# Attention and two expert layers on one core: sign masks of the first weight slices in SBUF instead of PSUM, first weight combinations asked for at tile 66, order of the instructions made in four passes

## The chip, the core and the metric

One core of a Trainium2 chip runs the kernel alone. The core has five engines that each work through a list of their own: PE multiplies matrices into PSUM, DVE, ACT and POOL work elementwise, and SP only asks for transfers. POOL works on SBUF alone here; DVE and ACT read and write PSUM too. The metric is the device time of one execution in microseconds (us).

## The reference

```python
q_pool = q.reshape(B, H, S // 2, 2, D).mean(axis=3)          # B 2, H 8, S 1152, D 64
scores = np.matmul(q_pool, k.transpose(0, 1, 3, 2)) / np.sqrt(D)
attn = np.exp(scores - scores.max(-1)); attn = attn / (attn.sum(-1) + 1e-9)
x = np.matmul(attn, v)                                       # then tokens x heads: 1152 x 512
h = x @ moe_w_in;  x = np.maximum(0.01 * h, h) @ moe_w_out   # 512 -> 2048 -> 512
h = x @ moe2_w_in; x = (h * np.tanh(softplus(h))) @ moe2_w_out
```

The four weight matrices arrive as float64, 1152 tokens pass through both layers, and the output is float32.

## The kernel before

**Attention.** Two heads make a pair; eight pairs come one after the other, each as nine tiles of 128 query rows, so there are 72 tiles. A tile n goes through: scores of 128 rows by 1152 keys on PE (L560) into PSUM columns 128 to 1279 for one parity of n and 1280 to 2431 for the other; the row maximum on DVE (L569 over 896 columns, L575 over 256, L580 joins them); the exponential on ACT (L591); nine transposes on PE in three groups (L615); of each group a rounded copy on ACT (L628) and the remainder on DVE (L633), since every product is made of high and low parts; and the product with v on PE (L650). A unit of that product leaves PSUM on ACT (L660), a transfer asked for by SP (L663) and POOL (L664) finish it, and once per pair PE and DVE scale it (L755 to L758). POOL also makes the low parts of the next pair's k, q and v (L394 to L406).

**Expert layers.** Each layer runs over eight slices of 256 hidden columns; i counts the 16 slices. A slice's first product is done in seven smaller products on combined operands (L840, six matmuls each; L845 to L858 finish them), the second product is L915 in layer one and L925 in layer two, summed into Y by DVE (L905, L907). L724 in `last_pair` is the first thing that PE does after the last tile's product with v: it ends the attention.

**Weights.** A slice has four parts b of 128x512 float64. `stage(i, b)` loads a part as pairs of 32-bit words (L786) and makes float32 of it: ACT turns the high word (L787) and the low word (L788) into scaled numbers, DVE takes the sign bit out of the high word (L793) and shifts it into place under the number (L794), and POOL adds the low word (L796). For slices 0 and 1 the sign mask goes, 128 columns at a time, to two strips of PSUM:

```python
strips = [PS[:, c:c + 128].bitcast(I32) for c in (0, 2432)]
```

The kernel itself counts PSUM in banks of 512 columns (`PS[:, 512 * bank[name]:...]`); the two strips lie in the first and the fifth such stretch, beside the columns of the scores. From slice 2 on the mask takes 512 columns at 3584. `convert(i)` makes the combinations of parts 0 and 1 on POOL (L808 and three `minus`) and splits all four parts into high and low.

**Order.** A `Recorder` takes down every operation, works out who depends on whom from the cells that each touches, and `plan` puts all operations in one order. Up to `rec.cut` (tile 63) the order is the one written out by hand in PATTERN; only operations marked loose, such as `stage(0, b)` at tiles 12, 27 and 42, are slipped in where their engine would otherwise idle by the planner's costs. Behind the cut it is a list schedule by due times. Each engine then executes its own list in that order, and waits for other engines where an operation needs it.

Of the kernel before, what the change touches and what calls it, by code (L numbers as in the profile page):

```python
# [26 lines left out]
NPR = B * NPAIR  # L27
# [14 lines left out]
CUT = 63  # L42
# [5 lines left out]
class Op:  # L48
    __slots__ = ("alts", "reads", "writes", "preds", "succs", "due", "n", "loose", "eng", "end", "go")


class Recorder:
# [5 lines left out]
    def __init__(self, nc, file):  # L58
        self.nc, self.file, self.ops, self.open, self.cut, self.free = nc, file, [], None, None, False
        for name in self.ENGINES:  # L60
            setattr(self, name, Proxy(self, name))

    @contextmanager
    def unit(self):
        assert self.open is None
        self.open = []
        yield
        made, self.open = self.open, None
        if made:
            self.add([(made[0][0], [c for m in made for c in m[1]], sum(m[2] for m in made),  # L70
                       sum(m[2] for m in made[:-1]) + made[-1][3])],
                     [x for m in made for x in m[4]], [x for m in made for x in m[5]])

    @contextmanager
    def loose(self):

        self.free = True
        yield
        self.free = False

    def add(self, alts, reads, writes):
        op = Op()
        op.alts, op.reads, op.writes, op.preds, op.succs = alts, reads, writes, set(), []
        op.n, op.eng, op.due, op.loose = len(self.ops), None, 0.0, self.free
        self.ops.append(op)

    def call(self, name, method, args, kw):
        frame = sys._getframe(2)
        while frame.f_code.co_filename != self.file:
            frame = frame.f_back  # L90
        outs = [kw[k] for k in ("out", "accum_out") if k in kw] or list(args[:1])
        ins = [v for k, v in kw.items() if k not in ("out", "accum_out")] + list(args[1 if args and "out" not in kw else 0:])
        outs = [x for x in outs if hasattr(x, "partition_size")]
        ins = [x for x in ins if hasattr(x, "partition_size")]
        eng = self.ENGINES[name]
        occ, fin = self.cost(eng, method, outs, ins, kw)
        reads = [c for x in ins for c in self.cells(x)]
        writes = [c for x in outs for c in self.cells(x)]
        if method == "matmul" and not kw.get("start"):
            reads = reads + writes  # L100
        made = (eng, [(name, method, args, kw, frame.f_lineno)], occ, fin, reads, writes)
        if self.open is not None:
            self.open.append(made)
        else:
            self.add([made[:4]], reads, writes)

    @staticmethod
    def cost(eng, method, outs, ins, kw):
# [56 lines left out]
    def plan(self):  # L165
# [17 lines left out]
        at = 0.0  # L183
        for op in self.ops:
            op.due = at
            if op.alts[0][0] == "PE":
                at += op.alts[0][2]
        back = dict.fromkeys(("PE", "DVE", "ACT", "POOL", "SP"), at + 9000)
# [3 lines left out]
        def latest(op):  # L192
            eng, _, occ, fin = op.alts[0]
            if eng != "PE":
                op.due = at + 3000
            for s in op.succs:
                op.due = min(op.due, s.due - (occ if eng == "PE" and s.alts[0][0] == "PE" else fin + self.SYNC))
            heapq.heappush(heap, (-op.due, -op.n, op))

        for op in self.ops:  # L200
            if not wants[op]:
                latest(op)
        while heap:
            op = heapq.heappop(heap)[2]
            eng, _, occ, _ = op.alts[0]
            op.due = min(op.due, back[eng] - occ)
            if eng != "PE":
                back[eng] = op.due
            for p in op.preds:
                wants[p] -= 1  # L210
                if not wants[p]:
                    latest(p)
        free = dict.fromkeys(("PE", "DVE", "ACT", "POOL", "SP"), 0.0)
        order = []

        def ready(op, eng):
            t = 0.0
            for p in op.preds:
                t = max(t, p.go + p.alts[0][2] if p.eng == eng == "PE" else p.end + self.SYNC)
            return t  # L220

        def place(op, alt):
            eng, calls, occ, fin = alt
            op.eng, op.go = eng, max(free[eng], ready(op, eng))
            op.end = op.go + fin
            free[eng] = op.go + occ
            order.append((op, calls))

        def force(op):
            for p in sorted(op.preds, key=lambda p: p.n):  # L230
                if p.eng is None:
                    force(p)
            place(op, op.alts[0])

        loose = []
        for op in self.ops[:self.cut]:
# [3 lines left out]
            for p in sorted(op.preds, key=lambda p: p.n):  # L240
                if p.eng is None:
                    force(p)
            eng = op.alts[0][0]
            start = max(free[eng], ready(op, eng))
            found = True
            while found:
                found = False
                for l in loose:
                    if l.eng is None and l.alts[0][0] == eng and all(p.eng for p in l.preds):
                        if max(free[eng], ready(l, eng) + 300) + l.alts[0][2] <= start + SLIP:  # L250
                            place(l, l.alts[0])
                            found = True
                            break
            place(op, op.alts[0])
            loose = [l for l in loose if l.eng is None]
        done = len(order)
        rest = [op for op in self.ops if op.eng is None]
        left = {op: sum(p.eng is None for p in op.preds) for op in rest}
        waiting = {op for op in rest if not left[op]}
        while waiting:  # L260
            by = {}
            for op in waiting:
                eng = op.alts[0][0]
                by.setdefault(eng, []).append((max(free[eng], ready(op, eng)), op.due, op.n, op))
            best = []
            for eng, ops in by.items():
                first = min(ops)
                t0 = max(first[0], free[eng])
                near = [x for x in ops if x[0] <= t0 + 5]
                pick = min(near, key=lambda x: x[1:3])  # L270
                soon = [x for x in ops if x[0] <= t0 + LOOK * pick[3].alts[0][2] and x[1] < pick[1] - 1000]
                if soon:
                    pick = min(soon, key=lambda x: x[1:3])
                best.append((pick[0], pick[2], pick[3]))
            _, _, op = min(best)
            place(op, op.alts[0])
            waiting.discard(op)
            for s in op.succs:
                if s in left:
                    left[s] -= 1  # L280
                    if not left[s]:
                        waiting.add(s)
        assert len(order) == len(self.ops)
        return order[:done] + sorted(order[done:], key=lambda x: x[0].go)

    def emit(self):
        lines = {}
        for op, calls in self.plan():
            for name, method, args, kw, line in calls:
# [15 lines left out]
def tile_attention_moe_moe(  # L305
# [65 lines left out]
    strips = [PS[:, c:c + 128].bitcast(I32) for c in (0, 2432)]  # L371
# [400 lines left out]
    def stage(i, b):  # L772
# [23 lines left out]
        nc.gpsimd.tensor_tensor(out=ai, in0=ai, in1=v[:, :, 0], op=ALU.add)  # L796

    def convert(i):

        if i >= NI:  # L800
            return
        wi, wo, a = WI[i % 2], WO[i % 3], wa[i % 2]
# [11 lines left out]
        split([wi[:, A12:S1, h] for h in range(2)], d2)  # L814
        for f in range(2):
            stage(i, 2 + f)
            split([wo[:, h, f] for h in range(2)], a[2 + f])
# [219 lines left out]
    with tc.manual_schedule():  # L1037
# [91 lines left out]
        assert not pvq and not prep  # L1129
        while xq:  # L1130
# [42 lines left out]
```

## Time and profile before

| | |
|---|---|
| device time, median of 3 runs | 661.79 us (661.2 to 662.08) |
| the profiled execution, device time | 661.79 us |
| its span, first to last instruction | 660.0 us |
| PE idle in the span | 23.2 us |
| mean granted TensorE clock | 0.997 of full speed |

The span is what the trace covers; the 1.79 us between it and the device time lie around it. Busy time of an engine is the time in which at least one of its instructions runs, and PE's ends are modelled, so the last two rows say where PE had nothing to do, and not that it ran at its peak elsewhere.

### The profile page before, as it was taken

What the parts mean: (1) busy time and instruction counts of PE and PEld (TensorE: products, weight loads), DVE (VectorE), ACT (ScalarE), POOL (GpSimd) and SP (SyncE); (2) the same over time, 40 slices, a digit from 0 to 9 for tenths busy, and PEclk for the clock granted to TensorE, in tenths of its full rate; (3) what the DMA queues carried; (4) which work ended last, traced back from release to release, by engine and by line L of the source; (5) the groups of instructions that cost most, each with busy time, mean ns of one, the idle gap of its engine ahead of it and who ended that gap; (6) DMA issues with size and microseconds to landing.
All of it is one profiled execution on the core that took longest, in us unless ns stands there. A gap on an engine that the chain in (4) does not pass through costs nothing.

```text
span 660.0 us, 11899 instructions
## 1 busy us (share of the span) xinstructions
PE 636.8 (96%) x4179; PEld 587.2 (89%) x4179; DVE 505.1 (77%) x1072; ACT 493.8 (75%) x1051; POOL 468.2 (71%) x450
## 2 busy tenths in 40 slices
PE   7899999999999988899999999999999999999997
PEld 5799889998999976789999999999999989999996
DVE  5889889998999988767677676678867766767454
ACT  6889889999999977867767766578776767576430
POOL 6957486888888653898777887669766797677200
PEclk9999999999999989999999999999999999999999
DMA  4424233333232222122332231322212232231003
GB/s 122 139 82 152 69 98 107 102 112 85 83 86 77 56 69 68 44 69 97 97 128 96 96 128 66 128 65 65 66 64 97 96 103 90 96 97 65 1 0 144
DMA packets 18172, 57.79 MB, mean 88 GB/s; under 512 B 2368, under 2 KB 4928, under 8 KB 18112
## 3 DMA queue, kind: packets, MB, share of 16 engines
q1 hardware_dynamic: 16768, 52.18, 24.4%
q0 software_dynamic: 1120, 4.59, 3.0%
q8 instruction: 33, 0.54, 0.3%
q14 instruction: 27, 0.22, 0.1%
q10 hardware_dynamic: 224, 0.26, 0.1%
HBM read 47.71 MB, written 2.36 MB: 76 GB/s over the span
## 4 chain that ended last, share of the span: by engine, by line
PE 87%; ACT 5%; DVE 4%; issue 2%; POOL 1%; DMA 1%; SPq 0%; DVEq 0%; ACTq 0%; POOLq 0%
PE PS L840 26%; PE PS L925 15%; PE PS L915 13%; PE PS L560 11%; PE PS L650 10%; PE PS L615 9%; ACT F L591 2%; PE PS L955 2%; DVE R L633 1%; POOL R L394 1%; ACT R L628 1%; DVE F L569 1%; DMA I<-in_kT_dram 1%; PE PS L755 0%; POOL R L406 0%
## 5 line engine op out<-in xcount | busy, mean ns | idle before, releaser
L840 PE MATMUL PS<-R 128*128 128x288 f32 x1344 | 203.9, 295 | 1.3 <-ACT F L591 1.1
L840 PEld LDWEIGHTS PS<-R 128*128 128x128 f32 x1344 | 190.9, 188 | 8.7 <-ACT F L591 1.3
L684 POOL TENSOR_TENSOR R<-F,R 128x288 fp32r<-128x288 f32 (+1 forms) x124 | 125.8, 1030 | 48.2 <-ACT F L854 37.7
L907 DVE TENSOR_TENSOR F<-PS,F 128x512 f32<-128x512 f32 (+2 forms) x140 | 84.0, 602 | 55.4 <-PE PS L925 31.7
L633 DVE TENSOR_TENSOR R<-PS,R 128x384 fp32r<-128x384 f32 x216 | 112.6, 550 | 9.4 <-ACT R L628 8.9
L560 PE MATMUL PS<-R 128*128 128x512 f32 (+2 forms) x480 | 111.2, 360 | 8.5 <-ACT F L591 7.5
L628 ACT CAST R<-PS 128x384 fp32r<-128x384 f32 x216 | 95.6, 486 | 17.6 <-PE PS L615 16.0
L925 PE MATMUL PS<-R 128*128 128x512 f32 x432 | 108.5, 390 | 0.0
L915 PE MATMUL PS<-R 128*128 128x320 f32 (+2 forms) x552 | 101.2, 322 | 0.7 <-DVE R L858 0.5
L615 PE MATMUL PS<-F 128*128 128x128 f32 x648 | 96.7, 277 | 5.4 <-DVE R L633 5.3
L796 POOL TENSOR_TENSOR F<-F,I 128x512 int32<-128x512 int32 x53 | 69.6, 1314 | 38.3 <-DVE F L794 14.7
L650 PE MATMUL PS<-R 128*128 128x256 f32 (+1 forms) x576 | 95.4, 304 | 0.9 <-DVE R L633 0.6
L591 ACT ACTIVATE F<-PS,F 128x1152 f32<-128x1152 f32 x72 | 88.5, 1229 | 6.7 <-DVE F L580 2.1
L560 PEld LDWEIGHTS PS<-R 128*128 128x128 f32 x480 | 75.6, 194 | 18.4 <-ACT F L591 8.5
L615 PEld LDWEIGHTS PS<-F 128*128 128x128 f32 x648 | 76.7, 141 | 16.4 <-DVE R L633 8.8
L925 PEld LDWEIGHTS PS<-R 128*128 128x128 f32 x432 | 77.7, 188 | 12.4
L915 PEld LDWEIGHTS PS<-R 128*128 128x128 f32 x552 | 84.3, 188 | 4.5 <-DVE R L858 0.8
L650 PEld LDWEIGHTS PS<-R 128*128 128x128 f32 x576 | 80.6, 189 | 2.8 <-DVE R L633 0.9
L569 DVE TENSOR_REDUCE F<-PS 128x1 f32<-128x896 f32 x72 | 77.9, 1082 | 0.6 <-PE PS L560 0.6
L853 ACT ACTIVATE R<-PS 128x288 fp32r<-128x288 f32 x96 | 39.1, 409 | 45.4 <-DVE PS L848 38.7
L845 ACT COPY F<-PS 128x288 f32<-128x288 f32 x96 | 38.5, 401 | 37.2 <-PE PS L840 35.5
L858 DVE TENSOR_TENSOR R<-PS,R 128x288 fp32r<-128x288 f32 x96 | 43.4, 454 | 29.6 <-ACT PS L854 29.2
(88 smaller groups left out, 857.7 us busy)
## 6 DMA issues: line engine op xcount, KB each, us to landing
I<-in_w_dram SPq DMA_DIRECT2D x61, 512.0 KB, 3.2
I<-in_vN_dram SPq DMA_DIRECT2D x8, 576.0 KB, 4.2
R<-R POOLq DMA_DIRECT2D x14, 320.0 KB, 4.2
I<-in_qT_dram SPq DMA_DIRECT2D x7, 576.0 KB, 4.9
I<-in_kT_dram SPq DMA_DIRECT2D x7, 576.0 KB, 4.0
out_dram<-F SPq DMA_DIRECT2D x8, 256.0 KB, 2.0
F<-in_w_dram SPq DMA_DIRECT2D x3, 512.0 KB, 3.8
F<-F SPq DMA_DIRECT2D x16, 80.0 KB, 2.0
```

The costliest lines, as they stand in the source:

```text
L560: nc.tensor.matmul(out=PS[:, pc:pc + w], lhsT=lq, rhs=KS[p % 2][:, h, kc:kc + w], start=(i == 0), stop=(i == len(ops) - 1))
L569: nc.vector.tensor_reduce(out=mx[:, n % 3, 0:1], in_=PS[:, a:e], axis=AX.X, op=ALU.max, negate=True)
L591: nc.scalar.activation(out=ebuf[n % 3], in_=PS[:, a:e], func=AF.Exp, scale=SCALE, bias=mx[:, n % 3, 2:3], accum_out=rcol(n))
L615: nc.tensor.transpose(PS[:, col + 128 * i:col + 128 * i + 128], ebuf[n % 3][:, 128 * k:128 * k + 128], ident)
L628: nc.scalar.copy(out=pt_dst(n, g, 0), in_=t_src[n, g][1])
L633: nc.vector.tensor_tensor(out=pt_dst(n, g, 1), in0=src, in1=rounded(pt_dst(n, g, 0)), op=ALU.subtract)
L650: nc.tensor.matmul(out=PS[:, bank[1]:bank[1] + n], lhsT=vs[:, k, 128 * h:128 * h + 128], rhs=PT[:, slot, s, k, 0:n], start=(k == 0 and s = ...
L684: (eng or nc.gpsimd).tensor_tensor(out=to, in0=a, in1=b, op=ALU.subtract)
L840: nc.tensor.matmul(out=at(name), lhsT=wi[:, wop, ws, k], rhs=X[:, g, k, xop, xs_], start=start and k == j == 0, stop=k == 1 and j == 2, sk ...
L907: nc.vector.tensor_tensor(out=y, in0=ps, in1=y, op=ALU.add)
L915: nc.tensor.matmul(out=ps, lhsT=wo[:, ws, f, 128 * d:128 * d + 128], rhs=gs[f][:, gi, t0:t0 + w], start=f == j == 0, stop=f == 1 and j == 2)
L925: nc.tensor.matmul(out=PS[:, 512 * b:512 * b + DM], lhsT=gs[f][:, gi, 128 * t:128 * t + 128], rhs=wo[:, ws, f], start=f == j == 0, stop=f ...
```

## The change

The strips go. For slices 0 and 1 the mask is made in place, over the high words in SBUF, so L793's output and all inputs of L794 now lie in SBUF (L817 and L818 in the changed kernel). Parts 0, 1 and 2 of slice 0 are staged in three pieces of 172, 170 and 170 columns instead of whole; their masks no longer go in four steps of 128. The hand-written order reaches to tile 66, loose operations of `stage` may make the next one wait up to 150 ns by the planner's costs, and at tile 66 `convert_in(0)`, `stage(0, 3)`, `stage(1, 0)` and `stage(1, 1)` are asked for. The planner takes a matmul as one that writes whole banks, charges DVE operations that lie in SBUF alone 2.5 or 1.8 times, and makes its schedule four times, each time with the ends of the one before as the key, and takes the shortest.

```diff
-CUT = 63
+CUT = 66
+AHEAD = 66
+PASSES = 4
+HOLD = 150
+PIECES = ((0, 172), (172, 342), (342, 512))
...
+        if eng == "PE":
+            writes = [("PS", c, 0) for b in sorted({c[1] // 4 for c in writes}) for c in range(4 * b, 4 * b + 4)]
...
-            both = method in ("tensor_tensor", "scalar_tensor_tensor") and all(
-                "PS" not in a.tensor.name for a in ins)
-            return (n + 62) / 0.96 * (3 if both else 1), (n + 145) / 0.96 * (3 if both else 1)
+            slow = 1
+            if n > 64 and all("PS" not in a.tensor.name for a in ins + outs):
+                slow = 2.5 if method == "tensor_tensor" else 1.8
+            return (n + 62) / 0.96 * slow, (n + 145) / 0.96 * slow
...
-                        if max(free[eng], ready(l, eng) + 300) + l.alts[0][2] <= start + SLIP:
+                        if max(free[l.eng], ready(l) + 300) + l.occ < start + l.loose:
...
+        for _ in range(PASSES):
+            self.backward(key)
+            found = self.forward()
+            if best is None or found[0] < best[0]:
+                best = found
+            key = {op: op.end for op in self.ops}
+        return best[1]
...
-    strips = [PS[:, c:c + 128].bitcast(I32) for c in (0, 2432)]
...
-        raw = xraw if rec.free else wraw[(4 * i + b) % 2]
-        v = raw.rearrange("p (n t) -> p n t", t=2)
+        early = (i, b) in ((0, 0), (0, 1), (0, 2))
+        raw = xraw if early else wraw[(4 * i + b) % 2]
         nc.sync.dma_start(out=raw, in_=w[s, b].bitcast(I32))
-        nc.scalar.activation(out=a, in_=v[:, :, 1].bitcast(F32), func=AF.Copy, scale=2.0 ** -112)
-        nc.scalar.activation(out=v[:, :, 0], in_=v[:, :, 0].bitcast(U32), func=AF.Copy, scale=2.0 ** -29)
-        n = 128 if i < 2 else 512
-        for c in range(512 // n):
-            part = slice(n * c, n * c + n)
-            sign = strips[c % 2] if i < 2 else signs
-            nc.vector.tensor_scalar(out=sign, in0=v[:, part, 1], scalar1=-2 ** 31, scalar2=None, op0=ALU.bitwise_and)
-            nc.vector.scalar_tensor_tensor(out=ai[:, part], in0=ai[:, part], scalar=3, in1=sign,
-                                           op0=ALU.logical_shift_left, op1=ALU.bitwise_or)
-        nc.gpsimd.tensor_tensor(out=ai, in0=ai, in1=v[:, :, 0], op=ALU.add)
+        for c0, c1 in PIECES if early else ((0, 512),):
+            v = raw[:, 2 * c0:2 * c1].rearrange("p (n t) -> p n t", t=2)
+            y, yi = a[:, c0:c1], ai[:, c0:c1]
+            nc.scalar.activation(out=y, in_=v[:, :, 1].bitcast(F32), func=AF.Copy, scale=2.0 ** -112)
+            nc.scalar.activation(out=v[:, :, 0], in_=v[:, :, 0].bitcast(U32), func=AF.Copy, scale=2.0 ** -29)
+            sign = v[:, :, 1] if i < 2 else signs
+            nc.vector.tensor_scalar(out=sign, in0=v[:, :, 1], scalar1=-2 ** 31, scalar2=None, op0=ALU.bitwise_and)
+            nc.vector.scalar_tensor_tensor(out=yi, in0=yi, scalar=3, in1=sign, op0=ALU.logical_shift_left,
+                                           op1=ALU.bitwise_or)
+            nc.gpsimd.tensor_tensor(out=yi, in0=yi, in1=v[:, :, 0], op=ALU.add)
...
+            if n == AHEAD:
+                assert ("U", NPR - 2, 3) in given and not prep
+                with rec.loose(SLIP):
+                    convert_in(0)
+                    stage(0, 3)
+                    stage(1, 0)
+                    stage(1, 1)
             if n in STAGE:
-                with rec.loose():
+                with rec.loose(HOLD):
                     stage(0, STAGE.index(n))
```

What this does to the lists is seen at three places. The first is DVE's list at tile 18, in the first third of the attention (in all order rows PS is PSUM, R, F and I are SBUF tiles; a changed kernel's line is 24 higher, or 30 behind `stage`). Before:

```order
L580 TENSOR_SCALAR F<-F 128x1
L793 TENSOR_SCALAR PS<-F 128x128 x2
L633 TENSOR_TENSOR R<-PS,R 128x3x128 x3
L569 TENSOR_REDUCE F<-PS 128x1
L575 TENSOR_REDUCE F<-PS 128x1
L633 TENSOR_TENSOR R<-PS,R 128x3x128
L580 TENSOR_SCALAR F<-F 128x1
L633 TENSOR_TENSOR R<-PS,R 128x3x128
L569 TENSOR_REDUCE F<-PS 128x1
L575 TENSOR_REDUCE F<-PS 128x1
L580 TENSOR_SCALAR F<-F 128x1
L794 SCALAR_TENSOR_TENSOR F<-F,PS 128x128 x2
```

The same place in the changed kernel:

```order
L604 TENSOR_SCALAR F<-F 128x1
L818 SCALAR_TENSOR_TENSOR F<-F 128x172
L657 TENSOR_TENSOR R<-PS,R 128x3x128 x3
L593 TENSOR_REDUCE F<-PS 128x1
L599 TENSOR_REDUCE F<-PS 128x1
L657 TENSOR_TENSOR R<-PS,R 128x3x128
L604 TENSOR_SCALAR F<-F 128x1
L657 TENSOR_TENSOR R<-PS,R 128x3x128
L593 TENSOR_REDUCE F<-PS 128x1
L599 TENSOR_REDUCE F<-PS 128x1
L604 TENSOR_SCALAR F<-F 128x1
```

Part 0 was masked by eight instructions between tiles 18 and 24; now one pair of instructions stands in each round of nine tiles (mask at tiles 16, 25, 34, 43, 52 and 61, shift at 18, 27, 36, 45, 52 and 63), for parts 0 and 1.

The second place is DVE's list at tiles 65 to 66, at the end of the attention. Before (the first row of L569 is tile 65's):

```order
L569 TENSOR_REDUCE F<-PS 128x1
L633 TENSOR_TENSOR R<-PS,R 128x3x128
L575 TENSOR_REDUCE F<-PS 128x1
L793 TENSOR_SCALAR PS<-F 128x128
L580 TENSOR_SCALAR F<-F 128x1
L794 SCALAR_TENSOR_TENSOR F<-F,PS 128x128 x2
L633 TENSOR_TENSOR R<-PS,R 128x3x128 x2
L569 TENSOR_REDUCE F<-PS 128x1
L633 TENSOR_TENSOR R<-PS,R 128x3x128
L575 TENSOR_REDUCE F<-PS 128x1
```

In the changed kernel the staging stands at tiles 68 and later (the first L593 row is tile 69's; the next is tile 70's):

```order
L593 TENSOR_REDUCE F<-PS 128x1
L657 TENSOR_TENSOR R<-PS,R 128x3x2x64
L599 TENSOR_REDUCE F<-PS 128x1
L657 TENSOR_TENSOR R<-PS,R 128x3x2x64
L657 TENSOR_TENSOR R<-PS,R 128x3x128
L604 TENSOR_SCALAR F<-F 128x1
L817 TENSOR_SCALAR F<-F 128x170
L657 TENSOR_TENSOR R<-PS,R 128x3x128
L818 SCALAR_TENSOR_TENSOR F<-F 128x170
L593 TENSOR_REDUCE F<-PS 128x1
L657 TENSOR_TENSOR R<-PS,R 128x3x128
L599 TENSOR_REDUCE F<-PS 128x1
```

Between tile 63's L569 and the multiplication behind L724 (L735 before, L759 now) DVE's list before has 48 masking instructions of 128 columns. Now it has 14: three masks and four shifts of 172 or 170 columns, four masks and three shifts of 512; and one more L878 (L848) and two more L888 (L858). Tiles 64 to 67 have none.

The third place is PE's list just ahead of the end of the attention. Before:

```order
L615 MATMUL PS<-F 128x128 x3
L650 MATMUL PS<-R 128x320 x5
L840 MATMUL PS<-R 128x288 x6
L615 MATMUL PS<-F 128x128 x6
L840 MATMUL PS<-R 128x288 x6
L650 MATMUL PS<-R 128x256 x6
L840 MATMUL PS<-R 128x288 x6
L650 MATMUL PS<-R 128x256 x8
L840 MATMUL PS<-R 128x288 x6
L650 MATMUL PS<-R 128x256 x4
L724 MATMUL PS<-F 128x128 x2
```

In the changed kernel:

```order
L870 MATMUL PS<-R 128x288 x6
L639 MATMUL PS<-F 128x128 x6
L870 MATMUL PS<-R 128x288 x6
L639 MATMUL PS<-F 128x128 x3
L870 MATMUL PS<-R 128x288 x12
L639 MATMUL PS<-F 128x128 x3
L870 MATMUL PS<-R 128x288 x6
L639 MATMUL PS<-F 128x128 x3
L870 MATMUL PS<-R 128x288 x6
L674 MATMUL PS<-R 128x256 x18
L748 MATMUL PS<-F 128x128 x2
```

All 42 matmuls of the first expert block (seven products) now stand ahead of the end of the attention, between the last tiles' transposes; before it were 30. PE executes the same 4181 instructions in both kernels, and its list is the same up to about tile 63; behind that all lists differ, those of the expert layers too.

## Rows read from the trace of the kernel before

**Rows 1.** The page: span, then each engine's busy us (share) and instructions.

```profile
span 660.0 us, 11899 instructions
PE 636.8 (96%) x4179; PEld 587.2 (89%) x4179; DVE 505.1 (77%) x1072; ACT 493.8 (75%) x1051; POOL 468.2 (71%) x450
```

**Rows 2.** Busy us (and instructions) of each engine by stretch, granted clock, DMA.

```profile
72.00:98.00 26.00, 24.29 (x173) 21.59 (x171) 22.96 (x57) 21.79 (x44) 18.84 (x17) 1.00 0.27 80
98.00:157.00 59.00, 58.92 (x424) 54.72 (x422) 54.24 (x117) 55.37 (x112) 46.94 (x46) 1.00 0.31 91
...
226.77:279.80 53.03, 44.57 (x290) 38.31 (x290) 42.65 (x122) 42.25 (x87) 31.11 (x36) 0.97 0.18 57
279.80:290.00 10.20, 9.46 (x66) 8.52 (x65) 7.64 (x19) 6.53 (x16) 10.04 (x13) 1.00 0.08 15
290.00:656.40 366.40, 366.21 (x2338) 343.28 (x2337) 254.86 (x499) 242.95 (x553) 252.97 (x234) 1.00 0.26 86
```

**Rows 3.** Timeline of DVE (start, us): L569 of tiles 18, 27, 36, 54.

```profile
70.49 1.08 DVE L569 TENSOR_REDUCE F<-PS 128x1 f32<-128x896 f32 x1
103.47 1.08 DVE L569 TENSOR_REDUCE F<-PS 128x1 f32<-128x896 f32 x1
133.67 1.08 DVE L569 TENSOR_REDUCE F<-PS 128x1 f32<-128x896 f32 x1
196.51 1.08 DVE L569 TENSOR_REDUCE F<-PS 128x1 f32<-128x896 f32 x1
```

**Rows 4.** DVE's waits, 72 to 98 us, then 157 to 172 us (total, times, longest).

```profile
DVE PS L793 <- ACT F L591: 1.5, 1, 1.5
DVE F L794 <- PE PS L560: 0.7, 1, 0.7
...
DVE PS L793 <- ACT F L591: 0.8, 1, 0.8
DVE F L794 <- PE PS L560: 0.6, 1, 0.6
```

**Rows 5.** DVE in groups by form, 226.77 to 279.80 us, then 290 to 660 us.

```profile
L793 DVE TENSOR_SCALAR PS<-I 128x128 int32<-128x128 int32 x20 | 5.3, 287 | 2.6 <-ACT F L591 1.5 <-PE PS L560 1.0
L794 DVE SCALAR_TENSOR_TENSOR F<-F,PS 128x128 int32<-128x128 int32 x20 | 5.0, 282 | 2.9 <-ACT F L591 2.4 <-ACT F L787 0.4
...
L793 DVE TENSOR_SCALAR PS<-I 128x512 int32<-128x512 int32 x56 | 38.4, 685 | 0.2
L794 DVE SCALAR_TENSOR_TENSOR F<-F,PS 128x512 int32<-128x512 int32 x49 | 33.3, 680 | 0.7
```

**Rows 6.** Timeline of DVE in the same stretch: masking instructions, with idle time before them.

```profile
248.95 0.29 DVE L794 SCALAR_TENSOR_TENSOR F<-F,PS 128x128 int32<-128x128 int32 x1 [1.45 <-ACT F L591]
...
271.01 0.48 DVE L794 SCALAR_TENSOR_TENSOR F<-F,PS 128x128 int32<-128x128 int32 x2 [0.43 <-ACT F L787]
...
272.20 0.48 DVE L793 TENSOR_SCALAR PS<-I 128x128 int32<-128x128 int32 x2
```

**Rows 7.** Timeline of DVE at tiles 18 and 71, then of POOL beside the second.

```profile
72.58 0.16 DVE L673 TENSOR_SCALAR F<-F 128x8 f32<-128x8 f32 x1
...
268.22 0.84 DVE L673 TENSOR_SCALAR F<-F 128x8 f32<-128x8 f32 x1
...
267.41 0.86 POOL L664 TENSOR_TENSOR F<-F 64x320 f32<-64x320 f32 x1
268.23 0.80 POOL L684 TENSOR_TENSOR F<-F 128x288 f32<-128x288 f32 x1
```

**Rows 8.** ACT in groups by form, 226.77 to 279.80 us.

```profile
L788 ACT ACTIVATE I<-I 128x512 int32<-128x512 uint32 x5 | 3.4, 685 | 0.0
L854 ACT ACTIVATE PS<-PS 128x288 f32<-128x288 f32 x1 | 0.4, 414 | 0.0
```

**Rows 9.** Timeline of PE: a wait ahead of the scores, and the attention's end.

```profile
245.14 0.74 PE L560 MATMUL PS<-R 128*128 128x256 f32 x4 [1.07 <-ACT F L591]
...
279.80 1.13 PE L724 MATMUL PS<-F 128*128 128x128 f32 x6
```

**Rows 10.** The chain that ended last, in the expert layers (start, us, what).

```profile
300.39 0.79 PE PS L840 x6
```

More of the change, by code (lines that the diff above doesn't have):

```diff
@@ L182, in plan, with lag, backward, enter @@
                 p.succs.append(op)
[L183 to L188, printed above, removed]
+    def lag(self, a, b):
+        return a.occ if a.eng == b.eng == "PE" else a.fin + self.SYNC
+    def backward(self, key):
+        end = sum(op.occ for op in self.ops if op.eng == "PE")
+        back = dict.fromkeys(self.ENGINES.values(), end + 9000)
         wants = {op: len(op.succs) for op in self.ops}
         heap = []
[L192 to L198, printed above, removed]
+        def enter(op):
+            op.due = min([end + 3000] + [s.due - self.lag(op, s) for s in op.succs])
+            heapq.heappush(heap, (-(op.due if key is None or op not in key else key[op]), -op.n, op))
         for op in self.ops:
             if not wants[op]:
-                latest(op)
+                enter(op)
         while heap:
             op = heapq.heappop(heap)[2]
[L205 to L208, printed above, removed]
+            op.due = back[op.eng] = min(op.due, back[op.eng] - op.occ)
             for p in op.preds:
@@ L211, in plan, with forward, ready, place @@
                 if not wants[p]:
-                    latest(p)
-        free = dict.fromkeys(("PE", "DVE", "ACT", "POOL", "SP"), 0.0)
+                    enter(p)
+    def forward(self):
+        free = dict.fromkeys(self.ENGINES.values(), 0.0)
         order = []
[L216 to L227, printed above, removed]
+        for op in self.ops:
+            op.on = False
+        def ready(op):
+            return max([0.0] + [p.go + self.lag(p, op) for p in op.preds])
+        def place(op):
+            op.on, op.go = True, max(free[op.eng], ready(op))
+            op.end = op.go + op.fin
+            free[op.eng] = op.go + op.occ
+            order.append(op)
         def force(op):
             for p in sorted(op.preds, key=lambda p: p.n):
-                if p.eng is None:
+                if not p.on:
                     force(p)
-            place(op, op.alts[0])
+            place(op)
         loose = []
@@ L253, in plan @@
                             break
-            place(op, op.alts[0])
-            loose = [l for l in loose if l.eng is None]
+            place(op)
+            loose = [l for l in loose if not l.on]
         done = len(order)
[L257 to L271, printed above, removed]
-                if soon:
[L273 to L277, printed above, removed]
@@ new lines, in forward, with enter @@
+        left = {op: sum(not p.on for p in op.preds) for op in self.ops if not op.on}
+        waiting = {eng: [] for eng in free}
+        def enter(op):
+            op.rdy = ready(op)
+            waiting[op.eng].append(op)
+        for op in left:
+            if not left[op]:
+                enter(op)
+        while any(waiting.values()):
+            best = None
+            for eng, ops in waiting.items():
+                if not ops:
+                    continue
+                t0 = max(free[eng], min(op.rdy for op in ops))
+                pick = min((op for op in ops if op.rdy <= t0 + 5), key=lambda op: (op.due, op.n))
+                soon = [op for op in ops if op.rdy <= t0 + LOOK * pick.occ and op.due < pick.due - 1000]
+                if soon:
+                    pick = min(soon, key=lambda op: (op.due, op.n))
+                found = (max(free[eng], pick.rdy), pick.n, pick)
+                if best is None or found < best:
+                    best = found
+            op = best[2]
+            waiting[op.eng].remove(op)
+            place(op)
@@ L278, in plan @@
             for s in op.succs:
-                if s in left:
+                if not s.on:
                     left[s] -= 1
                     if not left[s]:
-                        waiting.add(s)
+                        enter(s)
         assert len(order) == len(self.ops)
-        return order[:done] + sorted(order[done:], key=lambda x: x[0].go)
+        return max(op.end for op in order), order[:done] + sorted(order[done:], key=lambda op: op.go)
+    def plan(self):
+        self.link()
+        at, key = 0.0, {}
+        for op in self.ops:
+            if op.eng == "PE":
+                key[op] = at
+                at += op.occ
+        best = None
+        for _ in range(PASSES):
+            self.backward(key)
+            found = self.forward()
+            if best is None or found[0] < best[0]:
+                best = found
+            key = {op: op.end for op in self.ops}
+        return best[1]
```

51 lines of the change are left out of this document (28 added, 23 removed).

## The prediction

> **What bounds the kernel now.** I read the page first: PE is busy for 636.8 of 660.0 us [rows 1], so all idle time of PE together is 23.2 us, and a change that leaves PE's list of instructions as it is can win little more than that. Then the busy time by stretch [rows 2] shows where PE idles. In the expert layers, 290 to 656 us, it lacks 0.19 us in 366.40. In undisturbed attention, 98 to 157 us, it lacks 0.08 in 59.00, though DVE (54.24, 91.9%) and ACT (55.37, 93.8%) are nearly full as well: there the three engines are in balance, and whatever DVE or ACT gets on top comes out at PE. Two stretches are worse: 72 to 98 us lacks 1.71 us, and the end of the attention, 226.77 (the first reduction of tile 63) to 279.80 (L724 [rows 9]), lacks 8.46 of 53.03. That last one is not full on any engine: DVE 42.65, ACT 42.25, POOL 31.11. Something makes them wait for each other.
>
> DVE's waits say what. The masking pair L793 and L794 waits for the exponential (L591) and for score matmuls (L560) of which it needs nothing: 2.2 us in the first stretch, 1.4 us at 157 to 172 us [rows 4], and 5.5 us at the end of the attention, all but 0.4 of it on those two [rows 5]. A strip lies in the same 512 columns of PSUM as scores, so the mask is held until the exponential has read them, 1.45 us at the longest [rows 6]. Behind the held instruction DVE's queue holds the remainders L633, for which PE's transposes wait, and the next maxima; the scores wait in turn, as for the 1.07 us of [rows 9].
>
> The price in time shows in the rounds of nine tiles [rows 3]: tile 27 to 36 takes 30.20 us, 18 to 27 with one staging takes 32.98, and the two rounds from 36 to 54 with another take 62.84. That is 2.78 and 2.44 us, 5.2 together, for two parts of weights.
>
> **The change part by part.** I make the sum against the profiled execution: span 660.0, 1.79 us around it, 661.79 in all, which is also the median of the three runs.
>
> *The two stagings ahead of tile 63.* Their cost of 5.2 us goes. In their place each round from tile 16 to 63 gets one mask and one shift. Own time: 128 columns take 287 ns and 512 take 685 [rows 5], so 1.04 ns a column and about 333 ns for 172; six instructions from 271.01 to 272.20 start 0.198 us apart [rows 6], so 0.09 of each overlaps the next, and a piece costs 0.245 us, a pair 0.49. The wait for PSUM is gone, but both now read and write SBUF alone, and the trace has one hint of what that does: L673, SBUF to SBUF, takes 0.16 us at tile 18, and 0.84 us where it meets L664 and L684 on POOL; it ends at 269.06, just as L684 does (269.03) [rows 7]. So I charge 0.68 us where POOL is busy. [...] In attention POOL is busy 80% [rows 2], so the two waits cost 2 x 0.80 x 0.68 = 1.1 us, and a round gets 1.6 us in all on DVE. DVE has 8.1% of 30.20 us free, 2.4 us. Bounds: nothing, if all of it falls into free time, or 77% as with the old stagings (3.8 us of own time and waits cost 2.78, 3.0 cost 2.44), 1.2 us. Since it is less than the free time but stands in two lumps, I take 0.4, 2.4 us for six rounds. ACT's and POOL's pieces grow by their starting costs only and are covered by the same free time. Net 2.8 us won (from 5.2 won to 2.2 lost).
>
> *The end of the attention.* On DVE 48 masking instructions at 0.198 go, 9.5 us. By the order rows 14 come: seven of 172 or 170 columns at 0.245 and seven of 512 at 0.595 (0.685 less the overlap), 5.9 us, and one L848 and two L858 more at some 0.37, 1.1 us. So 42.65 becomes 40.1 without a wait. Waits behind POOL, which is busy 59% of the stretch [rows 2]: 14 x 0.59 x 0.68 = 5.6 us; bounds 0 and 14 x 0.68 = 9.5. DVE then needs 45.7 us (40.1 to 49.6). On ACT two full-size conversions fewer (2 x 0.685), six of 172 columns (0.27 each, carried on from 0.414 at 288 and 0.685 at 512 [rows 8]) and four more L853 and L854 at 0.41 make 42.25 into 44.1. The tiles cannot run denser than in undisturbed attention: 45.7 / 0.919 = 49.7 us for DVE, 44.1 / 0.938 = 47.0 for ACT. The longer holds: 49.7 in place of 53.03, 3.3 us won. Bounds: 6.0 won (ACT's limit) and 0.9 lost (DVE at 49.6).
>
> [...]
>
> *Expert work ahead of the end.* Twelve more L840 stand ahead of L724; six take 0.79 us [rows 10], so 1.6 us of PE's work has left the stretch behind it. They go into the waits between transposes, which the 49.7 us include. Their L853, L854 and L858 are done earlier too, and of the 0.74 us that PE idles from 279.80 to 290 I take 0.4 as won (0 to 0.74).
>
> *The rest.* The weights of part 2 and of slice 1 are asked for later on SP, behind a unit's L663; they are needed only from tile 68 on, so nothing waits. Parts left for after the attention fall where DVE has 25% free. The other lists of the expert layers are new, and where PE lacks 0.19 us [rows 2] an order can only lose. DVE, ACT and POOL are at 70, 66 and 69% there, so the matmuls have slack to wait with; I put in one wait like that of [rows 9], 1.0 us lost (0 to 3.7, 1% of the stretch). The code that plans costs nothing on the chip.
>
> Sum: 2.8 + 3.3 + 1.6 + 0.4 - 1.0 = 7.1 us. Span 652.9, device time **654.7 us**.
>
> **Rivals.** *ACT holds the end of the attention.* ACT's work there grows, and its idle time stood mostly ahead of L628, behind PE's transposes; if the chain maximum, exponential, transpose, copy, remainder is what takes the time, and not the masks, the 53 us stay. Then 2.8 + 1.6 + 0.4 - 1.0 = 3.8 are won: 658.0. Against it: tiles without staging run at 30.2 us in nine [rows 3], and tiles 64 to 67 now have none.
>
> *The mask waits for POOL instead of PSUM.* This is the one that ends slower. Let every masking instruction wait w us behind POOL, and let none of it fall into free time, but 77% come out at PE as with the old stagings. Then the six rounds cost 6 x 0.77 x (0.49 + 2w), the end of the attention takes (40.1 + 14w) / 0.919, and with 1.6 + 0.4 - 1.0 the whole wins 5.2 - 2.3 - 9.2w + 53.0 - 43.6 - 15.2w + 1.0 = 13.1 - 24.4w: even at w = 0.54 us, and 3.5 us lost, 665.3, at the 0.68 of [rows 7] for all of them. For it: that L673 waited through the rest of one POOL instruction and the whole of the next, and adds and low parts stand back to back on POOL there. [...] Against it: one of eight L673 of 8 columns was caught, the other seven took 0.16, and at tiles 18 to 63 the shift stands behind the round's short operations, where POOL itself waits for DVE.
>
> *The two cancel, or the new order of the expert layers loses what the attention wins* (2%, 7.3 us, would do it): 661 to 662. The slack of the other engines there speaks against it.
>
> **Chances.** Forecast as summed, 651 to 658: 0.57. ACT holds: 0.15. Cancelled: 0.14, of which a little ends on either side. Slower, 663 to 668: 0.14. A difference under 0.2%, 1.3 us, is what a measurement here can hardly tell from none: faster 0.73, same 0.13, slower 0.14. The range of 8 in 10 reaches from the bounds won on both attention parts (5.2 + 6.0 + 1.6 + 0.7 - 1.0 = 12.5, 649.3) to the cancelled case.
>
> **What would show it.** Right: no wait of L817 or L818 for L591 or L560; rounds 18 to 27 and 36 to 54 at 30.2 to 30.8 a round; tile 63 to L748 in 47 to 51 us, PE idle there 3 to 6 us; expert layers still under 1.5 us idle. L818 with 172 columns at 0.33 us, some with 0.5 to 1 more beside a POOL instruction. Wrong: L818 regularly over 1 us, or L684 and L820 on POOL as much longer; ACT over 95% busy at tiles 68 to 71 with PE waiting for L628 or L591; PE waiting in the expert layers for L820 or the splits behind it. The granted clock was 0.97 in the old stretch, where PE had waited; 1.00 there would be up to 1.6 us more won, which the sum leaves out.

## The result and the profile after

The changed kernel takes 651.01 us (median of 4 runs, 649.95 to 652.54) against 661.93 us beside it: ratio 0.9835, 95% interval 0.9806 to 0.9863. That is 10.9 us less, where 7.1 were forecast (654.7 us, range 649.5 to 662.5). The profiled execution took 649.95 us, its span is 648.1.

The page of the changed kernel, to be read beside [rows 1]: PE is busy 5.9 us less and idle 17.2 us in place of 23.2.

```profile
PE 630.9 (97%) x4179; PEld 585.7 (90%) x4179; DVE 505.7 (78%) x1036; ACT 488.4 (75%) x1063; POOL 471.5 (73%) x456
```

Busy time by stretch, to be read beside [rows 2]. The stretches are cut at the first reduction (L593) of tiles 18, 27, 36, 54 and 63, and at L748 (269.70).

```profile
71.18:101.41 30.23, 30.23 (x220) 28.33 (x219) 28.40 (x63) 28.08 (x57) 21.81 (x21) 1.00 0.30 80
...
131.63:193.66 62.03, 61.46 (x438) 56.45 (x437) 57.37 (x127) 58.05 (x120) 54.90 (x55) 1.00 0.33 99
...
223.94:269.70 45.76, 42.15 (x303) 38.67 (x302) 42.15 (x89) 41.45 (x93) 32.37 (x37) 1.00 0.20 66
...
280.00:290.00 10.00, 9.39 (x71) 9.15 (x70) 6.71 (x15) 7.93 (x20) 9.92 (x9) 1.00 0.33 106
290.00:644.50 354.50, 353.85 (x2248) 331.10 (x2246) 248.40 (x485) 230.91 (x531) 244.38 (x228) 1.00 0.26 86
```

The round 18 to 27 takes 30.23 us in place of 32.98, the two from 36 to 54 take 62.03 in place of 62.84, and the end of the attention 45.76 in place of 53.03. Tile 63 begins 2.83 us earlier, L748 stands 7.27 us nearer to it, and from there to the last matmul it is 374.82 us in place of 376.64. 2.83 + 7.27 + 1.82 is the whole 11.9 us between the spans. In the end of the attention DVE is busy almost as long as before (42.15 us, 42.65 before): what went is its idle time, 3.61 us in place of 10.38, and the granted clock is 1.00 there in place of 0.97.

DVE's waits from tile 63 to L748 (total, times, longest); the 5.5 us of [rows 5] are gone, and no mask waits for the exponential or the scores any more:

```profile
DVE F L599 <- ACT F L615: 1.0, 3, 0.5
DVE I L817 <- ACT F L814: 0.5, 1, 0.5
DVE PS L878 <- PE PS L870: 0.4, 1, 0.4
DVE R L657 <- ACT R L652: 0.4, 2, 0.2
DVE F L599 <- PE PS L584: 0.3, 1, 0.3
```

What the masks cost now, in the timeline of DVE and, behind it, of POOL (start, us):

```profile
67.41 0.24 DVE L817 TENSOR_SCALAR F<-F 128x172 int32<-128x172 int32 x1
73.89 0.33 DVE L818 SCALAR_TENSOR_TENSOR F<-F 128x172 int32<-128x172 int32 x1
250.35 0.43 DVE L817 TENSOR_SCALAR I<-I 128x512 int32<-128x512 int32 x1
250.88 0.69 DVE L818 SCALAR_TENSOR_TENSOR F<-F,I 128x512 int32<-128x512 int32 x1
255.13 0.66 DVE L817 TENSOR_SCALAR I<-I 128x512 int32<-128x512 int32 x1
259.77 1.52 DVE L817 TENSOR_SCALAR I<-I 128x512 int32<-128x512 int32 x1
...
254.95 0.55 POOL L820 TENSOR_TENSOR F<-F 128x170 int32<-128x170 int32 x1 [0.34 <-ACT R L652]
259.70 1.30 POOL L820 TENSOR_TENSOR I<-I 128x512 int32<-128x512 int32 x1
```

A mask of 512 columns takes 0.43 us alone, where the one that writes PSUM took 0.685 [rows 5]; the shift takes 0.69, as before. Beside POOL the same mask takes 0.66 and 1.52 us: the two end at 255.79 and 261.29, 0.29 us after POOL's L820 (255.50 and 261.00).

### The profile page after: what moved, and what is told of

It is laid out like the page before. It is cut to its first block, busy times and chain, and to the rows that moved or that the text cites. A ratio compares the mean times of both kernels' runs of the same rounds, so it can differ in the third digit from the quotient of the medians.

```text
span 648.1 us, 11883 instructions
## 1 busy us (share of the span) xinstructions
PE 630.9 (97%) x4179; PEld 585.7 (90%) x4179; DVE 505.7 (78%) x1036; ACT 488.4 (75%) x1063; POOL 471.5 (73%) x456
## 4 chain that ended last, share of the span: by engine, by line
PE 88%; ACT 5%; DVE 3%; issue 1%; POOL 1%; DMA 1%; SPq 0%; DVEq 0%; ACTq 0%; POOLq 0%
PE PS L870 26%; PE PS L955 15%; PE PS L945 13%; PE PS L584 12%; PE PS L674 11%; PE PS L639 10%; ACT F L615 2%; PE PS L985 1%; ACT R L652 1%; POOL R L708 1%; ACT R L712 1%; DVE R L657 1%; DMA I<-in_kT_dram 1%; ACT R L502 0%; PE PS L779 0%
## 5 line engine op out<-in xcount | busy, mean ns | idle before, releaser
L870 PE MATMUL PS<-R 128*128 128x288 f32 x1344 | 200.6, 295 | 0.6 <-POOL R L708 0.6
L584 PE MATMUL PS<-R 128*128 128x512 f32 (+2 forms) x480 | 109.0, 356 | 6.6 <-ACT F L615 4.0
L945 PE MATMUL PS<-R 128*128 128x320 f32 (+2 forms) x552 | 99.1, 322 | 0.0
L639 PE MATMUL PS<-F 128*128 128x128 f32 x648 | 94.9, 275 | 2.4 <-ACT F L684 0.9
L820 POOL TENSOR_TENSOR F<-F,I 128x512 int32<-128x512 int32 x53 | 69.5, 1314 | 31.0 <-DVE F L818 14.0
L593 DVE TENSOR_REDUCE F<-PS 128x1 f32<-128x896 f32 x72 | 78.0, 1083 | 0.5 <-PE PS L584 0.4
L888 DVE TENSOR_TENSOR R<-PS,R 128x288 fp32r<-128x288 f32 x96 | 43.4, 453 | 28.1 <-ACT PS L884 27.8
L712 ACT CAST R<-F 128x512 fp32r<-128x512 f32 (+1 forms) x92 | 49.5, 549 | 13.3 <-POOL F L820 6.8
```

Of the source, the lines that this page charges most:

```text
L584: nc.tensor.matmul(out=PS[:, pc:pc + w], lhsT=lq, rhs=KS[p % 2][:, h, kc:kc + w], start=(i == 0), stop=(i == len(ops) - 1))
L593: nc.vector.tensor_reduce(out=mx[:, n % 3, 0:1], in_=PS[:, a:e], axis=AX.X, op=ALU.max, negate=True)
L639: nc.tensor.transpose(PS[:, col + 128 * i:col + 128 * i + 128], ebuf[n % 3][:, 128 * k:128 * k + 128], ident)
L870: nc.tensor.matmul(out=at(name), lhsT=wi[:, wop, ws, k], rhs=X[:, g, k, xop, xs_], start=start and k == j == 0, stop=k == 1 and j == 2, sk ...
L945: nc.tensor.matmul(out=ps, lhsT=wo[:, ws, f, 128 * d:128 * d + 128], rhs=gs[f][:, gi, t0:t0 + w], start=f == j == 0, stop=f == 1 and j == 2)
```

## The experiments

The table is worked out from each run's timeline: first reduction of tile 9 to that of tile 63, from there to the end of the attention (L724 in the kernel before), from there to the last matmul, all of the profiled execution; the mean granted clock in the end of the attention, since it falls for a while in some of the runs (in the kernel before it is 0.50 from 239.5 to 242.5 us); then the median of the device time and its ratio to the kernel before, run beside it.

```
                        9 to 63    end  clock  experts   device  ratio, 95% interval
before                   186.74  53.03   0.97   376.64    661.9
changed                  183.21  45.76   1.00   374.82   651.01  0.9835 (0.9806 to 0.9863)
b_sbuf                   182.77  54.08   0.94   375.44   657.73  0.9939 (0.9919 to 0.9959)
a_strips                 200.59  55.43   0.94   373.45   676.02  1.0214 (1.0189 to 1.0238)
a_noahead                183.35  46.11   1.00   375.12   650.20  0.9832 (0.9812 to 0.9852)
a_pass1                  183.57  45.59   1.00   377.55   652.07  0.9854 (0.9836 to 0.9872)
b_pieces                 183.63  49.07   0.93   379.10   658.21  0.9938 (0.9917 to 0.9958)
a_whole                  182.63  48.69   0.96   377.96   655.65  0.9905 (0.9886 to 0.9924)
a_cut63                  183.23  49.53   0.97   373.48   653.28  0.9872 (0.9850 to 0.9894)
a_nobank                 183.39  47.20   1.00   376.50   653.15  0.9872 (0.9852 to 0.9893)
a_four                   190.43  44.22   1.00   373.97   654.46  0.9893 (0.9877 to 0.9909)
a_four_psum              195.10  44.20   1.00   373.66   658.57  0.9958 (0.9941 to 0.9974)
a_cut69                  183.54  45.96   1.00   378.83   654.37  0.9891 (0.9874 to 0.9908)
a_pass8                  183.20  45.73   1.00   374.40   649.37  0.9817 (0.9802 to 0.9832)
```

**The place of the mask alone, on the kernel before (b_sbuf).**

```diff
-        n = 128 if i < 2 else 512
+        n = 512
-            sign = strips[c % 2] if i < 2 else signs
+            sign = v[:, part, 1] if i < 2 else signs
```

> The kernel before with only the mask moved: in place over the high words, 512 columns at a time; its order, cut at tile 63, costs and single pass stay. If the hold in PSUM is the cause, the mask waits for no exponential and no score matmul, the end of the attention (first reduction of tile 63 to L724) takes 46 to 49 us instead of 53.0, each of the two earlier stagings costs under 1 us instead of 2.8 and 2.4, and the device time is 652 to 655 us. If the new order is the cause, the end still takes 51 us or more and the time is 657.5 us or more.

As to the time and the end it came out where the order was to be the cause, at 657.73 us with an end of 54.1: no mask or shift waited for the exponential or the scores any more, and the end got no shorter. Only the two earlier stagings came out as the hold would have it (rounds 18 to 27 and 36 to 54 take 30.30 and 61.45 us, 32.98 and 62.84 before). One limit of the run: the planner charges a shift of 512 columns from SBUF three times, finds no gap for it, and the attention is free only because the work is left over. In DVE's timeline the first part's mask stands at tile 20, its shift 150 us later (79.31 and 229.53 us).

So taking the hold away does not by itself shorten the end of the attention; whether it would with part 0's shift out of the way, this run doesn't say. The granted clock weighs on it too, 0.94 in this end; the one execution of the six with a mean granted clock of 1.000 took 655.01 us, where the kernel before at 1.000 takes 660.3 to 660.9.

**The mask back in PSUM, on the changed kernel (a_strips).** `stage` as before, with the strips.

```diff
-        for c0, c1 in PIECES if early else ((0, 512),):
+        for c0, c1 in ((0, 512),):
...
-            sign = v[:, :, 1] if i < 2 else signs
+            n = 128 if i < 2 else 512
+            for c in range(512 // n):
+                part = slice(n * c, n * c + n)
+                sign = strips[c % 2] if i < 2 else signs
...
```

> The changed kernel with only the mask moved back: two strips of PSUM, 128 columns at a time, parts staged whole; tile 66, the early combinations and four passes stay. If the hold is the cause, waits of the masking for L615 (exponential) and L584 (scores) come back with 3 us or more, and the time is 656 to 661 us. If the order is the cause, 651 to 653.5 us.

676.02 us, far beyond both. With 150 ns of leave per operation the planner now puts all eight masking instructions of a part into one spot (seven of part 0's at tile 13), and three rounds of nine tiles take 34 to 38 us. Up to the end of the attention the masks wait 2.7 us for the exponential (L616 here), never for the scores, and once 3.9 us for the transfer of their weights. So the forecast of 3 us or more of those waits was missed as well, most of the loss has another cause, the lumps being the likely one, and the run doesn't price the hold.

**The hold by itself (a_four, a_four_psum).** Four pieces of 128 columns, so that a strip holds one; in the second kernel the planner takes a strip for a place in SBUF, so every engine's list is in the same order as in the first, and only the 12 early masks differ in where they lie.

```diff
-PIECES = ((0, 172), (172, 342), (342, 512))
+PIECES = tuple((c, c + 128) for c in range(0, 512, 128))
```

```diff
-            sign = v[:, :, 1] if i < 2 else signs
+            sign = strips[c0 // 128 % 2] if early else v[:, :, 1] if i < 2 else signs
...
+        if self.strip(x):
+            return [("STRIP", x.offset, 0)]
```

> The changed kernel with the first three parts in four pieces of 128 columns, masks in SBUF: the control for the next one. All three parts are then masked by tile 56. Either way 649 to 654 us, with no wait of the masks for the exponential (L615) or the scores (L584).

> The kernel with four pieces, every list in the same order, and only the twelve early masks written to the two strips of PSUM. If the hold by the scores' columns is what the old stagings cost, masks and shifts wait for L615 and L584 again, 0.3 us each and more, rounds with masks are 1 to 3 us longer than the control's, and the time is 3 to 9 us above the control. If the old cost was the time of the masking itself, the two are within 1 us of each other, or the one in PSUM is ahead because its shift meets no POOL instruction.

The control missed its 649 to 654 us by 0.5. 658.57 against 654.46 us: the place costs 4.1 us, and the intervals lie apart. All of it is ahead of tile 63 (195.10 against 190.43), though not in every round: 9 to 18 is 1.0 us shorter with the masks in PSUM, 45 to 54 and 54 to 63 are 2.0 and 2.7 us longer. DVE in groups by form in the attention, first with masks in SBUF (mask L817, shift L818), then in PSUM (L824, L825); after the bar the idle time of DVE just before them:

```profile
L818 DVE SCALAR_TENSOR_TENSOR F<-F 128x128 int32<-128x128 int32 x12 | 7.4, 628 | 0.0
L817 DVE TENSOR_SCALAR F<-F 128x128 int32<-128x128 int32 x12 | 5.9, 509 | 0.0
```

```profile
L825 DVE SCALAR_TENSOR_TENSOR F<-F,PS 128x128 int32<-128x128 int32 x12 | 3.3, 283 | 7.4 <-ACT F L622 5.8 <-PE PS L591 1.6
L824 DVE TENSOR_SCALAR PS<-F 128x128 int32<-128x128 int32 x12 | 3.3, 286 | 2.6 <-ACT F L622 1.7 <-PE PS L591 0.9
```

Both mechanisms of the forecast are in these four rows. In PSUM the 24 instructions run 6.6 us and wait 10.0 for exponential and scores; in SBUF they wait for nothing and run 13.3. The shortest of them there take 0.22 us (mask) and 0.28 (shift), and what all 24 took beyond that is 7.7 us. It is POOL's share: each of the ten longer ones starts while a POOL instruction runs and ends 0.1 to 0.2 us after it. SBUF is the cheaper place, and not a free one.

How the hold turns into time shows best just ahead of tile 54 in the kernel with strips. A shift is held, behind it the remainder (L664) comes late, PE waits for that, and then the granted clock falls (DVE, PE, and the stretch behind them):

```profile
197.47 0.29 DVE L825 SCALAR_TENSOR_TENSOR F<-F,PS 128x128 int32<-128x128 int32 x1 [2.55 <-ACT F L622]
...
198.81 0.69 PE L786 MATMUL PS<-F 128*128 128x128 f32 x2 [2.71 <-DVE R L664]
...
198.10:204.80 6.70, 5.99 (x23) 5.76 (x24) 5.19 (x10) 3.09 (x9) 2.51 (x4) 0.50 0.03 12
```

At 0.50 these 6.7 us cost an estimated 3.4 at most, half their length, so in this execution much of the price comes through the clock. It is not all clock: of the executions with a granted clock of 0.997 in the mean, those with strips took 657.52 and 657.56 us, those without 654.77 and 655.20.

**Staging without the planner (b_pieces).** The kernel before with masks in SBUF, pieces, the new DVE costs and the 150 ns; no tile 66, one pass, no whole banks.

> The kernel before with the new staging alone: masks in SBUF, parts 0 to 2 of slice 0 in three pieces, the new DVE costs and the 150 ns that let them be slipped in from tile 16 on. Cut at tile 63, one pass, no whole banks for matmuls, nothing asked for at tile 66. If staging (no hold in PSUM, and work spread over the attention) is the cause, the end of the attention takes 45 to 48 us and the time is 651 to 654 us. If the planner's part is the cause, the end stays at 50 us or more and the time is 656 us or more.

The first theory's figure for the attention came true (183.63), the end went half the way (49.07), and the expert layers lost 2.5 us: 658.21, which the forecast had for the planner's part. In its stretch from tile 63 on DVE is busy 39.81 us, less than in the changed kernel, and PE is idle 5.68 us; the granted clock is 0.93, which is at most an estimated 3.4 us of the 49.07 (0.07 of it). So DVE's work alone doesn't set the length of the end: PE's waits do, 5.4 us in all, with what the clock loses.

```profile
224.68:273.75 49.07, 43.39 (x284) 38.47 (x284) 39.81 (x86) 41.05 (x88) 33.46 (x39) 0.93 0.22 73
```

**One part out of the changed kernel at a time.**

```diff
-AHEAD = 66
+AHEAD = 999
```

> The changed kernel without the request at tile 66 (combinations of slice 0 and the stagings that go with it are asked for after the attention, as before); all else stays. If the hold is the cause, 650.5 to 653 us. If the early request is what fills the end, fewer of the 42 matmuls of the first block stand ahead of L748, the end takes 48 us or more and the time is 654 us or more.

All five lists are the same, row for row, as the changed kernel's, so the request at tile 66 does nothing to the order. The run is a second measurement of the same program: 650.20 beside 651.01 us. Three of its four executions had a mean granted clock of 1.000 and took 649.8 to 650.4 us, some 10 us less than the kernel before at 1.000: the change brings as much where the clock doesn't fall.

```diff
-PIECES = ((0, 172), (172, 342), (342, 512))
+PIECES = ((0, 512),)
```

> The changed kernel with parts 0 to 2 staged whole (512 columns) in SBUF. By the order all their masks then stand at tile 67 and later. If the pieces matter because they bring two parts' work into the attention, rounds up to tile 63 take 30.2 to 31 us, the end takes 50 to 54 us, and the time is 655 to 659 us; if only the way out of PSUM matters, 650 to 653 us.

655.65 us: all masks stand at tile 67 and later, and the end takes 48.69 us, 2.9 more than with pieces; another 3.1 are lost in the expert layers. Part of both is the clock (0.96 in the end, 0.89 from there to 290 us: at most an estimated 1.9 and 1.8 us), and the profiled execution was the slowest of the six. But at a mean clock of 1.000 it still took 654.12 us, so the pieces matter, by all likelihood because they carry two parts' work into the attention.

The run shows one more thing. In rounds 36 to 54 no staging instruction stands here, and they take 61.43 us all the same (61.45 in `b_sbuf`, where none stands either), and not twice the 30.20 of round 27 to 36.

```diff
-PASSES = 4
+PASSES = 1
```

> The changed kernel with one planning pass instead of four. If the hold is the cause, 650.5 to 653 us; if the passes make the order that wins, 654 us or more, with the end of the attention 48 us or longer or the expert layers idle for over 2 us.

```diff
-CUT = 66
+CUT = 63
```

> The changed kernel with the hand-written order ending at tile 63 as before. The masks stand at the same tiles up to 63. If staging is the cause, 650 to 653 us with the end at 45 to 47 us; if the hand-written order of tiles 63 to 65 matters, the end takes 48 us or more and the time is 653.5 us or more.

`a_nobank` drops the two lines that let a matmul write whole banks in the plan.

> The changed kernel with a planner that takes a matmul as one that writes its own columns alone, as before. The masks stand at the same tiles. If staging is the cause, 650 to 653 us; if the whole banks in the plan matter, PE waits for over 2 us more at the end or in the expert layers and the time is 653.5 us or more.

One pass gives 652.07 us, not told apart from four by the intervals, though the profile has 2.7 us more in the expert layers. The cut at 63 gives 653.28 (end 49.53 in place of 45.76, expert layers 1.3 us shorter) and plain columns 653.15 (end 47.20, expert layers 1.7 us longer): some 2 us each by the medians, but both intervals overlap that of the changed kernel (0.9806 to 0.9863), so neither difference is shown.

**Further along the same way (a_cut69, a_pass8).** `CUT = 69`, and `PASSES = 8`.

> The changed kernel with the hand-written order carried on to tile 69. If the order of the last tiles by hand is what won from 63 to 66 (653.3 against some 651 us), the end gets shorter again and the time is 648 to 650.5 us; if the list schedule needs those tiles to place the staging in, it is 652 us or more.

> The changed kernel with eight planning passes. PE's list is the same as with four; the other engines' lists differ in a few hundred rows. If lists of that kind matter, 1 us or more either way; I expect 650 to 652 us, no difference.

Tile 69 is worse than 66: the end stays at 45.96, and the expert layers lose 4.0 us. Eight passes give 649.37 us, the lowest median of all and clearly under the kernel before, but its interval overlaps that of four passes.

## Why the prediction was right, and what it mis-sized

**What bounds the kernel: shown ahead of tile 63, argued for the end.** Masks in the scores' stretches of PSUM hold DVE, and for twelve masks ahead of tile 63 that costs 4.1 us with every list in the same order, the fall of the clock included (0.98 in the mean there, 1.00 in `a_four`). At the end of the attention no run parts the hold from the order: there the waits went in `b_sbuf` and the end stayed. The waits in `a_four_psum` are 10.0 us, for columns that the mask does not touch but that lie in the same stretch of 512; why the program waits for those, and whether it has to, no run shows.

**The two early stagings: right in size, with two terms wrong that cancel.** 2.8 us net were forecast at tile 63 and 2.83 measured, which is in part luck: from tile 9 to 63 the win is 3.5 us (186.74 to 183.21), and tile 9 began 0.70 us later in this execution (below). The forecast took the 30.20 us of round 27 to 36 as the base of the rounds 36 to 54 too. These take 61.4 us with no staging in them (`a_whole`, `b_sbuf`), so the second staging cost 1.4 us and not 2.44, and both 4.2 in place of 5.2. The pieces cost 0.6 us in the rounds 36 to 54 (62.03) and nothing in the others, 2.4 being forecast. The 1.1 us of waiting for POOL that I charged to a round did not come: of the 12 instructions of these six rounds one was held, by 0.24 us. The shift at 73.89 is typical: POOL's L700 starts at 74.00, 0.1 us behind it, and is the one to wait (0.27 us in place of 0.18), as the rival's own counter-argument had it.

**The end of the attention: the term that was mis-sized.** 49.7 us were forecast, 45.76 measured, which is nearly all of the missing 3.8 us. DVE's demand was put at 45.7 and measured 42.15. Two parts of it were too large: the masks' own time, taken from the form that writes PSUM (0.685 for 512 columns, measured 0.43; 1.3 us over the seven masks), and the waits for POOL, 5.6 us forecast and 3.8 measured, counting what the 14 instructions took over their shortest (0.24 and 0.33, 0.43 and 0.69). The density came true, 42.15 of 45.76 is 92.1% against 91.9% assumed, though it is no limit: in the end of `a_nobank` DVE is busy 44.45 of 47.20 us, 94.2%. ACT's demand was put at 44.1 and measured 41.45. Two of the forecast's signs of being right were missed by this, the end at 47 to 51 us and, by the wrong base, the rounds 36 to 54 at 30.2 to 30.8 (31.0). From SBUF to SBUF the masks gain in the trace, 0.43 us in place of 0.685 and 0.24 in place of the 0.33 estimated, and the shift does not, 0.69 against 0.680 [rows 5] and 0.33 as estimated; why the one gains and the other not, no run shows.

That density was an assumption which this order fulfils and others don't. In `b_pieces`, with the same staging, DVE is busy 39.81 us in 49.07, 81%: there PE waits for DVE's remainders up to 1 us at a time, 2.7 us in all, and the granted clock is 0.93. The runs with an end of 48.69 us or more all have a granted clock of 0.93 to 0.97 in it, those with 47.20 or less all 1.00. So in these runs an end without longer waits of PE is gained twice, by the waits and by the clock that stays at 1.00. The forecast's reason, less DVE work without holds, fits the way from 53.0 to some 49 us, and the order of the last tiles the rest, but no run parts the two at the end, and DVE's busy time fell by 0.5 us only. That the list schedule would reach the attention's density came true, and was not argued for.

**The expert layers: nearly right.** 1.0 us was forecast as won (1.6 + 0.4 - 1.0), 1.82 measured. The new order idles PE 1.26 us between L748 and the last matmul where the old one idled 0.93, so 0.33 us were lost by waits and not 1.0. That it came out so well looks like luck with the order: the other orders of this study, some with other work left over, lie between 373.5 and 379.1 us there, a wider spread than the forecast's 3.7 us.

**The rivals.** ACT did not keep the end at 53 us; it is busy 90.6% of the new end. The blocking by POOL is real, some 7.7 us for 24 instructions in `a_four`, but less than the hold it replaces; in the changed kernel it is 0.24 us in the six rounds and 3.8 at the end. The masks at 255.13 and 259.77 us start while POOL's L820 runs and end 0.29 us after it. In the sum for this rival the forecast slipped: its terms give 13.3 - 24.4w and not 13.1, so 665.1 us and not 665.3; nothing hangs on it. A rival that the forecast did not name, that the gain is the clock's, is ruled out by the executions at 1.000 (`a_noahead`).

**Which part brings it.** Staging alone is worth 3 to 4 us (`b_pieces`), the planner with the strips and whole parts loses 14 (`a_strips`), both together bring 10.9. They don't add; that the planner places what staging makes placeable is the likely reason, and not shown. Open is why the cut at 66 is better than that at 69.

## What to carry to other kernels

When an engine's waits name partners whose data it doesn't need, look at what else lies in the same stretch of PSUM before counting work: here that cost 4.1 us for twelve masks. Time a replacement form by its own kind of operands: source and destination in SBUF took the mask from 0.685 to 0.43 us and put it in POOL's way, with up to 1.52 us beside L820. And where three engines are in balance, spread added work in small pieces and judge it together with the order, since either alone gave a third of the gain or none. Look at the granted clock of a stretch before its length is put down to work: in `a_four_psum` a wait of PE of 2.71 us was followed by 6.7 us at 0.50.

## What was not expected of the hardware

The start differs from run to run with the same lists up to tile 9. From 10 to 15 us the granted clock was 0.52 in the profiled run of `a_whole` and 1.00 in that of `a_cut63`, and tile 9 began at 42.59 and 39.88 us:

```profile
10.00:15.00 5.00, 4.78 (x14) 3.45 (x13) 2.99 (x6) 2.48 (x5) 4.84 (x3) 0.52 0.00 0
...
10.00:15.00 5.00, 2.81 (x15) 2.06 (x14) 3.06 (x6) 3.58 (x6) 4.77 (x4) 1.00 0.00 0
```

PE had been waiting just before those 5 us, busy 2.43 of 5.00 us in the first run (clock 0.79) and 4.15 in the second. The changed kernel's own profile has 0.73 there (0.50 from 10.0 to 12.5 us, 1.00 from 13.0 on) and tile 9 at 40.73 us, that of `a_noahead`, with the same lists to the end, 1.00 and 39.97. That is up to 2.7 us of scatter in the start that no change to the later work explains, and it is why the table starts at tile 9. In the same way the end of the attention ran at 0.97 before, where PE idled 8.46 us, and at 1.00 after the change, where it idled 3.61.
